# A filter's last chunk loaded as 128 half rows, fewer fillers ahead of the first transforms, and another fixed order

## The chip, the cores and the metric

The kernel runs on one core of one Trainium2 chip. The time is device microseconds of one execution, median of several. The kernel's engines are TensorE (PE, with its weight loads shown as PEld), VectorE (DVE), ScalarE (ACT), GpSimd (POOL) and SyncE (SP), which here only issues transfers; POOL issues transfers too, between its own arithmetic.

## The reference

A pre-norm block with two mixers over 2048 tokens (S) of 448 channels (D), all in bf16. The first is a gated long convolution, the second an MLP over the token axis.

```
def _A_ref(q, k, v, shift_k, ssm_k, ssm_D):
    k_shift = sum over t of k_pad[:, t:t+S] * shift_k[:, ks-1-t]     # 4 taps
    kv = k_shift * v
    kv_f = rfft2(pad(kv, 2S));  kf_f = rfft2(pad(ssm_k, 2S))          # over the token axis
    y = irfft2(kv_f * kf_f)[:, :S] + kv * ssm_D
    return q * y
def _B_ref(x, w1, b1, w2, b2):
    h = layernorm(x)
    u = gelu(einsum("bsd,sf->bdf", h, w1) + b1)
    return (einsum("bdf,fs->bds", u, w2) + b2).transpose(0, 2, 1)
h  = A_q + _A_ref(layernorm(A_q), k, v, shift_k, ssm_k, ssm_D)
h2 = h + _B_ref(layernorm(h), x, w1, b1, w2, b2)
```

The filter ssm_k is given channel by channel, 448 rows of 2048 samples; everything else has tokens as rows. F, the inner width of the MLP, is 1792.

## The kernel before

**Tiling.** Both Fourier transforms are matrix products in two stages, with a transposition between the stages done by transfers inside SBUF ("shuffles"). Tokens are split as 16 interleaved rows r with 128 positions each, so a tile is 128 partitions by 448 channels.

**Steps.** The builder functions write operations into a list; each operation has a name of the form step:number, and the steps are these.

- loads: all first transfers, on SP's queue (L885 on). loads.0 to loads.3 bring the filter's four chunks of 128, 128, 128 and 64 channel rows into KN (L887); loads.4 is the small shift kernel, loads.5 to 12 are quarters of k and v, loads.13 the vector D, loads.14 the two biases.
- tables: the cosine and sine tables, built from integers on DVE, ACT and POOL. tables.5 and tables.6 build E, the first stage's matrices, with three long DVE operations each (L844) and one on ACT. tables.7:0 to 7:3 are four integer operations on POOL (L854 three times, L858), 7:4, 7:6 and 7:7 are on DVE, 7:5 is a sine on ACT (L862), 7:8 to 7:11 are POOL's last steps (L871, L874). They give the second stage's matrices and masks.
- kv: kv.1 to kv.8 build transposes of k on PE (L966); kv.9 to kv.16 are the shift matmuls on PE (L992) followed by a DVE product with v (L1007).
- kT.2c+g: transposes of half g of filter chunk c, eight on PE (L1038) into one PSUM bank, and a copy to SBUF as :8 (L738 on ACT or L741 on DVE).
- dummy: matmuls on a constant tile that nobody reads (L1025): nine at the start (N_W0), and after each of the first three filter chunks N_WK of them, three, in one PSUM bank of their own.
- k1.0 to 15 and u1.0 to 15: the first stage of the transform of the filter and of kv: eight PE matmuls (L1059) and a copy (L1069, or L1067 with an addition of D on DVE), then after every second one three shuffles: :9 and :10 on POOL's queue, :11 on SP's (L1075). Every four steps share a slot of a ring of four; a slot is free once its shuffles have landed.
- k2, u2: the second stage, four matmuls (L1094) and one or two copies (L738, L739, L741, L742).
- i1: the product of the two spectra on DVE (L1160), the first inverse stage on PE (L1177), copies, and shuffles on POOL and SP (L1200; those of the last pair, i1.16, are issued at L1189).
- i2: the second inverse stage for 16 tiles (L1299, L1307 on PE), combined with q and the residual on DVE (L1318, L1326, L1336), layer norm statistics (L1342, L1345, L1374 on DVE, a power on POOL), and a scaling into Q, the MLP's input (L1385). i2.8 is that scaling for the first tile.
- mlp: the two products (L1432 and L1442 for the two halves of F, L1454 with w2), gelu on ACT (L1422), final additions on DVE (L1457). w1a and w1b (L1405, L1409) are the loads of w1's halves in four parts each.
- xload, xn, q, ct, ew, warm, bias: loads of x's rows and their statistics, transposes of the tables and more dummy matmuls.

**Order.** A fixed order for every engine is written out in ORDER, a list of such names for each of pe, act, dve, pool and sp. An engine issues its list in order, and SP's and POOL's lists are also the order of their transfer queues. Who copies what (ACT or DVE) is set by the list in which the copy stands. A planner walks these lists at build time and gives out the eight PSUM banks, the ring slots and the semaphores; whoever takes a bank waits for its last reader. Nothing is chosen at run time. Numbers as t0 and est below only serve that planner.

Of the kernel before, what the change touches and what calls it, by code (L numbers as in the profile page):

```python
# [13 lines left out]
        "dummy.0:1-9 kv.4:0-11 kv.3:0-7 kv.6:0-11 kv.5:0-7 kT.1:0-7 kT.0:0-3 kT.1:9-11 kT.0:4-7 kT.3:0-7 kT.2:0-3 "  # L14
        "kT.3:9-11 kT.5:0-7 kT.2:4-7 kT.5:9-10 kT.6:0-7 kT.7:0-7 bias.0:0 kT.5:11 kv.7:0-7 kv.2:0-3 k1.12:0-7 "
        "k1.8:0-7 k1.9:0-7 kv.2:4-11 kv.1:0-7 k1.10:0-7 k1.11:0-7 kT.4:0-7 kv.8:0-3 k1.13:0-7 k1.14:0-7 kv.8:4-11 "
        "kv.10:0-23 kv.12:0-23 kv.9:0-27 k1.4:0-7 k1.15:0-7 kv.11:0-27 u1.0:0-7 u1.1:0-7 k1.0:0-7 k1.1:0-7 u1.2:0-7 "
        "u1.3:0-7 kv.13:0-27 u1.4:0-7 k1.5:0-7 kv.14:0-23 k1.6:0-7 u1.6:0-7 u1.5:0-7 k1.2:0-7 kv.15:0-27 k1.7:0-7 "
        "u1.7:0-7 u1.8:0-7 u1.9:0-7 k1.3:0-7 k2.0:0-3 k2.1:0-3 k2.12:0-3 k2.13:0-3 k2.4:0-3 k2.5:0-3 kv.16:0-23 "
        "k2.9:0-3 k2.8:0-3 u1.10:0-7 u1.12:0-7 u1.13:0-7 u1.14:0-7 u1.11:0-7 u1.15:0-7 k2.2:0-3 k2.3:0-3 k2.7:0-3 "  # L20
        "k2.6:0-3 k2.10:0-3 k2.11:0-3 k2.14:0-3 k2.15:0-3 u2.0:0-3 u2.1:0-3 u2.12:0-3 u2.13:0-3 u2.8:0-3 u2.9:0-3 "
        "u2.6:0-3 u2.7:0-3 i1.1:1-7 i1.1:10-17 i1.1:8 i1.14:10-16 i1.14:1-7 i1.14:17 i1.14:8 i1.8:1-7 i1.8:10-16 "
        "i1.8:8 i1.8:17 ct0.0:0-7 u2.10:0-3 u2.11:0-3 i1.10:1 i1.10:10-17 i1.10:2-8 u2.5:0-3 u2.4:0-3 i1.12:1-8 "
        "i1.12:10-17 u2.3:0-3 u2.2:0-3 i1.6:1-8 i1.6:10-17 u2.14:0-3 u2.15:0-3 i1.4:9-15 i1.4:0-6 i1.4:16 i1.4:7 "
        "warm.12:0 warm.13:0 i1.16:1-7 i1.16:10-17 i1.16:8 ct.2:0-7 ct.1:0-7 ct.0:0-7 warm.0:0 warm.1:0 warm.2:0 "
# [557 lines left out]
def _build(nc, A_q, A_k, A_v, A_shift_k, A_ssm_k, A_ssm_D, B_w1, B_b1, B_w2, B_b2, out):  # L583
# [5 lines left out]
    Bsz, S, D = A_q.shape  # L589
    F = B_w1.shape[1]  # L590
    assert Bsz == 1 and S == 2048 and D == 448 and F == 1792 and A_shift_k.shape[-1] == 4
    R = 16
    NFC = F // 128
    EPS = 1e-5
    DB = 2 * D
# [42 lines left out]
    with ctx:  # L638
# [89 lines left out]
        T_KX = -27.67  # L728
        T_EW = -10.0
        T_CP, T_XL, T_WB = 39.11, -35.53, 156.06  # L730
        N_WZ, N_WI, N_W0, N_WK, N_WJ = 14, 0, 9, 3, 0

        def evac(dst, src, w, b, n, scale=None, engs=FX, r=(), est=None):

# [782 lines left out]
```

## Time and profile before

| | us |
|---|---|
| runs | 173.97, 173.15, 173.49; median 173.49 |
| the profiled execution, whole | 173.37 |
| its span | 171.6 |
| first load landed, last first load landed | 4.4, 19.5 |
| k2 starts | 34.7 |
| MLP starts | 81.4 |
| granted TensorE clock | 1.00 throughout |

The profile is of one execution. Times inside it count from the start of the span. A row of a timeline gives start, length, engine, line, operation, output and input, count, and in brackets the idle time of the engine ahead of it with whoever ended it. A window row gives for each engine the busy time and the number of instructions in that stretch. The chain of waits is followed back from the last instruction: at each step to what released it, or to the one before it on its engine. A busy PE here includes the dummy matmuls, so its share says little; what matters for each stage is which engine has no gap in it.

### The profile page before, as it was taken

What the parts mean: (1) busy time and instruction counts of PE and PEld (TensorE: products, weight loads), DVE (VectorE), ACT (ScalarE), POOL (GpSimd) and SP (SyncE); (2) the same over time, 40 slices, a digit from 0 to 9 for tenths busy, and PEclk for the clock granted to TensorE, in tenths of its full rate; (3) what the DMA queues carried; (4) which work ended last, traced back from release to release, by engine and by line L of the source; (5) the groups of instructions that cost most, each with busy time, mean ns of one, the idle gap of its engine ahead of it and who ended that gap; (6) DMA issues with size and microseconds to landing.
All of it is one profiled execution on the core that took longest, in us unless ns stands there. A gap on an engine that the chain in (4) does not pass through costs nothing.

```text
span 171.6 us, 3585 instructions
## 1 busy us (share of the span) xinstructions
PE 162.5 (95%) x1431; PEld 94.6 (55%) x1431; DVE 100.9 (59%) x187; ACT 92.6 (54%) x133; POOL 59.4 (35%) x152
## 2 busy tenths in 40 slices
PE   6989999989889999988999999999999999999994
PEld 2776745452324333533455455555567777777783
DVE  7998797879899999979997730000003133132231
ACT  3786978988999999978975816321210000000000
POOL 8345727564810696444898730000000000000000
PEclk9999999999999999999999999999999999999999
DMA  5999757676859776547989999980000111101111
GB/s 160 418 308 384 248 180 273 245 281 208 274 132 408 254 212 177 160 153 219 329 314 392 407 424 419 418 351 11 0 4 0 53 53 53 53 4 53 53 53 54
DMA packets 15628, 35.15 MB, mean 205 GB/s; under 512 B 3740, under 2 KB 9740, under 8 KB 15612
## 3 DMA queue, kind: packets, MB, share of 16 engines
q1 hardware_dynamic: 12468, 28.25, 45.3%
q0 software_dynamic: 2880, 6.49, 12.0%
q8 instruction: 11, 0.18, 0.4%
q10 hardware_dynamic: 264, 0.18, 0.3%
q14 instruction: 5, 0.04, 0.1%
HBM read 22.05 MB, written 1.84 MB: 139 GB/s over the span
## 4 chain that ended last, share of the span: by engine, by line
PE 67%; ACT 17%; DMA 7%; DVE 3%; POOL 2%; issue 2%; DVEq 0%; ACTq 0%
PE ps L1454 25%; ACT arena L738 13%; PE ps L1432 12%; PE ps L1442 12%; DMA arena<-arena 7%; PE ps L1025 3%; PE ps L1059 3%; PE ps L1094 3%; ACT arena L1069 3%; PE ps L966 3%; PE ps L1038 3%; PE ps L1299 2%; PE ps L992 2%; ACT arena L739 2%; POOL arena L1075 2%
## 5 line engine op out<-in xcount | busy, mean ns | idle before, releaser
L1457 DVE SCALAR_TENSOR_TENSOR arena<-ps,arena 128x448 bf16<-128x448 f32 (+2 forms) x17 | 11.1, 656 | 57.2 <-PE ps L1454 57.2
L1454 PE MATMUL ps<-arena 128*128 128x448 bf16 (+2 forms) x238 | 42.7, 342 | 0.0
L1454 PEld LDWEIGHTS ps<-arena 128*128 128x128 bf16 x238 | 33.3, 145 | 9.5
L738 ACT CAST arena<-ps 128x896 bf16<-128x896 f32 x30 | 24.5, 1006 | 0.3 <-PE ps L1094 0.2
L1432 PE MATMUL ps<-arena 128*128 128x448 bf16 x112 | 22.5, 353 | 0.6 <-DVE arena L1374 0.6
L1075 POOL DMA_DIRECT2D arena<-arena x32 | 17.5, 553 | 13.2 <-ACT arena L1069 9.9
L1069 ACT CAST arena<-ps 128x896 bf16<-128x896 f32 x23 | 19.5, 913 | 3.8 <-PE ps L1059 3.5
L1442 PE MATMUL ps<-arena 128*128 128x448 bf16 x112 | 21.4, 352 | 0.0
L1422 ACT ACTIVATE arena<-ps,arena 128x448 bf16<-128x448 f32 x14 | 8.2, 640 | 19.6 <-PE ps L1442 14.7
L1432 PEld LDWEIGHTS ps<-arena 128*128 128x128 bf16 x112 | 10.7, 98 | 11.3 <-DVE arena L1374 1.0
L1094 PE MATMUL ps<-arena 128*64 128x448 bf16 x128 | 15.1, 360 | 1.7 <-ACT arena L739 0.7
L1160 DVE TENSOR_TENSOR arena<-arena 128x1792 bf16<-128x1792 bf16 x16 | 16.6, 1085 | 0.3
L1442 PEld LDWEIGHTS ps<-arena 128*128 128x128 bf16 x112 | 11.0, 98 | 10.2
L1177 PE MATMUL ps<-arena 64*128 64x448 bf16 x128 | 14.7, 351 | 1.1 <-DVE arena L1160 0.7
L1059 PE MATMUL ps<-arena 128*32 128x448 bf16 x256 | 15.2, 355 | 0.5
L1200 POOL DMA_DIRECT2D arena<-arena x14 | 8.3, 596 | 13.2 <-ACT arena L738 13.2
L1094 PEld LDWEIGHTS ps<-arena 128*64 128x64 f16 x128 | 5.7, 108 | 10.3 <-ACT arena L738 3.2
L1177 PEld LDWEIGHTS ps<-arena 64*128 64x128 f16 x128 | 5.9, 94 | 9.7 <-DVE arena L1160 3.2
L738 ACT COPY arena<-ps 128x1024 bf16<-128x1024 bf16 (+2 forms) x9 | 8.3, 977 | 3.3 <-PE ps L966 2.8
L1007 DVE TENSOR_TENSOR arena<-ps,arena 128x512 bf16<-128x512 f32 (+1 forms) x16 | 9.0, 616 | 1.4 <-PE ps L992 1.4
L1354 ACT ACTIVATE arena<-arena 128x448 bf16<-128x448 f32 x14 | 8.0, 573 | 3.0 <-DVE arena L1326 2.9
L1059 PEld LDWEIGHTS ps<-arena 128*32 128x32 f16 x256 | 5.0, 95 | 7.9 <-ACT arena L1069 2.4
(96 smaller groups left out, 195.5 us busy)
## 6 DMA issues: line engine op xcount, KB each, us to landing
arena<-in_B_w_dram SPq DMA_DIRECT2D x8, 896.0 KB, 7.8
arena<-in_B_w_dram SPq DMA_DIRECT2D x2, 2048.0 KB, 17.6
arena<-arena SPq DMA_DIRECT2D x16, 224.0 KB, 3.0
arena<-arena POOLq DMA_DIRECT2D x32, 112.0 KB, 3.5
arena<-in_B_w_dram SPq DMA_DIRECT2D x2, 1536.0 KB, 20.1
arena<-arena POOLq DMA_DIRECT2D x14, 196.0 KB, 4.7
arena<-in_A_k_dram SPq DMA_DIRECT2D x4, 448.0 KB, 5.5
arena<-in_A_v_dram SPq DMA_DIRECT2D x4, 448.0 KB, 8.7
```

Of the source, the lines that this page charges most:

```text
L738: return e.copy(out=dst(), in_=src())
L1007: return e.tensor_tensor(out=v, in0=u.rearrange("p t (r d) -> p t r d", d=64), in1=v, op=ALU.mult)
L1059: op("pe", lambda e, W, b=b, r=r, q=q, x=x, c0=c0: e.matmul(PS[32 * q:32 * q + 32, b.slots[x], 0:D], E[:, 2 * r + x, c0:c0 + 32], src[:, r ...
L1069: return e.copy(out=dst, in_=Ppair(b)) if W == "act" else e.tensor_copy(out=dst, in_=Ppair(b))
L1075: shuf[tag].append(op(q_, lambda e, W, g=g, i=i, a=a, nu=nu, jh=jh: e.dma_start(T[a + i:a + i + 4 * nu - 3:4].rearrange("p (j k) c d -> p ...
L1094: op("pe", lambda e, W, b=bs[h], h=h, j=j, c=c, par=par: e.matmul(PS[64 * par:64 * par + 64, b.slots[c], 0:D], FW[:, 64 * c:64 * c + 64], ...
L1160: op("dve", lambda e, W, m=m, i=i: e.tensor_tensor(out=MR(m.slots[0]).rearrange("p (x y) d -> p x y d", x=2), in0=TU[:, i].unsqueeze(2).br ...
L1177: k = op("pe", lambda e, W, b=bs[h], m=ms[h], par=par, t=t, tab=tab, xy=xy, P=P: e.matmul(Pb(b, par), tab[P, :], MR(m.slots[0])[P, xy, :], ...
L1432: op("pe", lambda e, W, r=r, fc=fc, b=bs[fc]: e.matmul(Pb(b), W1A[:, r, 128 * fc:128 * fc + 128], Q[:, r, :], start=(r == 0), stop=(r == R ...
L1442: op("pe", lambda e, W, r=r, fc=fc, b=b: e.matmul(Pb(b), W1B[:, r, 128 * (fc - n0):128 * (fc - n0) + 128], Q[:, r, :], start=(r == 0), sto ...
L1454: op("pe", lambda e, W, r=r, fc=fc, b=b, d0=d0, d1=d1: e.matmul(Pb(b)[:, d0:d1], W2[fc // 7][:, fc % 7, r:S:R], G[:, fc, d0:d1], start=(fc ...
L1457: op("dve", lambda e, W, r=r, b=b, A=A, d0=d0, d1=d1: e.scalar_tensor_tensor(out=X[:, r, d0:d1], in0=Pb(b)[:, d0:d1], scalar=bm[:, r:r + 1 ...
```

## The change

Five things.

1. The filter's last chunk, 64 channel rows of 2048 samples, is loaded as 128 half rows of 1024 (row 2c holds the first half of channel c, row 2c+1 the second). For each r there are now two matmuls in place of one transpose: the half rows, 128 partitions by 64 samples, are the stationary operand, and every second column of the identity is the moving one, so one matmul gives positions 0 to 63 and the other 64 to 127. The result is f32 in PSUM (a whole bank of 512), where the transposes left bf16.
2. The fillers between the filter chunks: three after each of three chunks become one after the first alone. Four new ones (fill.0 to fill.3) have a PSUM bank each from the planner and no reader.
3. w1a.0, the first quarter of w1's first half, no longer waits for u1's shuffles but for a landed z shuffle (that of i1.8), and stands further back in SP's list, behind the last pair's shuffles.
4. Some copies change engine: k2.13's second, kT.4's, kv.6's, u1.9's, one of u2.13's and of u2.3's, and i2.98, go to DVE; bias.0's, k1.14's, kT.7's, u1.7's, one of u2.1's and of u2.5's, and i2.94, go to ACT.
5. All five lists are in another order. Among the moves: tables.5's first step is DVE's first long one; POOL's tables.7:0 to 7:3 move from before the first shuffle to between k1.11's and k1.13's, tables.7:8 to 7:11 to between k1.5's and u1.5's; k1.14 and k1.15 stand ahead of kv.9, kv.10 and kv.12 on PE; the loads start with a quarter of k and filter chunks 0 and 2; on DVE, i2.14 and i2.55 stand ahead of i2.8; on PE, i2.58 stands ahead of the MLP's first product.

The lists are cut here to the parts named above; the code is whole.

```diff
 "pe":
-  "dummy.0:1-9 kv.4:0-11 kv.3:0-7 kv.6:0-11 kv.5:0-7 kT.1:0-7 kT.0:0-3 kT.1:9-11 kT.0:4-7 kT.3:0-7 kT.2:0-3 "
-  "kT.3:9-11 kT.5:0-7 kT.2:4-7 kT.5:9-10 kT.6:0-7 kT.7:0-7 bias.0:0 kT.5:11 kv.7:0-7 kv.2:0-3 k1.12:0-7 "
-  "k1.8:0-7 k1.9:0-7 kv.2:4-11 kv.1:0-7 k1.10:0-7 k1.11:0-7 kT.4:0-7 kv.8:0-3 k1.13:0-7 k1.14:0-7 kv.8:4-11 "
-  "kv.10:0-23 kv.12:0-23 kv.9:0-27 k1.4:0-7 k1.15:0-7 kv.11:0-27 u1.0:0-7 u1.1:0-7 k1.0:0-7 k1.1:0-7 u1.2:0-7 "
+  "dummy.0:1-9 kv.5:0-6 kv.6:0-3 fill.0:0 kT.1:0-7 kT.1:9 kT.0:0-7 kv.6:4-11 kT.5:0-7 bias.0:0 kv.5:7 "
+  "fill.1:0 fill.2:0 fill.3:0 kv.4:0-11 kT.6:0-15 kT.7:0-15 kv.3:0-7 kT.3:0-7 kT.2:0-7 kv.7:0-7 k1.8:0-7 "
+  "k1.12:0-7 k1.9:0-7 kv.1:0-7 kv.2:0-3 k1.10:0-7 kv.2:4-11 k1.11:0-7 k1.13:0-7 kT.4:0-7 kv.8:0-3 k1.14:0-7 "
+  "k1.15:0-7 kv.8:4-11 kv.12:0-23 kv.9:0-27 kv.10:0-23 k1.4:0-7 kv.11:0-27 k1.0:0 u1.0:0-7 u1.1:0-7 k1.0:1-7 "
...
 "dve":
-  "xn.3:1 i2.4:0 i2.11:0 i2.5:0 i2.18:0 i2.6:0 i2.12:0 i2.21:0 i2.13:0 q.7:1 i2.8:0 i2.14:0 i2.55:0 i2.30:0 "
+  "i2.12:0 i2.6:0 i2.13:0 i2.18:0 i2.14:0 i2.21:0 i2.55:0 i2.8:0 i2.16:0 i2.34:0 i2.30:0 i2.43:0 i2.26:0 "
...
 "pool":
-  "tables.2:6 q.0:0-1 kv.0:1-2 tables.7:0-3 tables.7:8-11 kv.0:0 k1.9:9-10 k1.11:9-10 k1.13:9-10 k1.15:9-10 "
-  "u1.1:9-10 u1.3:9-10 k1.1:9-10 k1.5:9-10 u1.5:9-10 k1.3:9-10 k1.7:9-10 u1.7:9-10 u1.9:9-10 u1.13:9-10 "
+  "tables.2:3 tables.2:0 tables.2:7 tables.2:10 tables.2:8 tables.2:11 kv.0:0 kv.0:2 tables.2:6 k1.9:9-10 "
+  "k1.11:9-10 tables.7:2 tables.7:1 tables.7:0 tables.7:3 k1.13:9-10 k1.15:9-10 u1.1:9-10 k1.1:9-10 u1.3:9-10 "
+  "k1.5:9-10 tables.7:8 tables.7:10 tables.7:9 tables.7:11 u1.5:9-10 k1.3:9-10 k1.7:9-10 u1.7:9-10 u1.9:9-10 "
...
 "sp":
-  "loads.6:0 loads.8:0 loads.0:0 loads.1:0 loads.2:0 loads.3:0 loads.13:1 loads.14:0-1 loads.10:0 loads.5:0 "
-  "loads.11:0 loads.4:0-2 loads.12:0 loads.9:0 loads.7:0 k1.9:11 k1.11:11 k1.13:11 k1.15:11 u1.1:11 k1.1:11 "
+  "loads.8:0 loads.0:0 loads.2:0 loads.14:0 loads.6:0 loads.3:0 loads.1:0 loads.10:0 loads.4:2 loads.4:1 "
+  "loads.4:0 loads.5:0 loads.14:1 loads.11:0 loads.7:0 loads.9:0 loads.13:1 loads.12:0 k1.13:11 k1.15:11 "
...
-  "w1a.0:0 xload.3:0 xload.2:0 ct0.1:0 i1.1:20 i1.1:22 ct0.1:1 ct0.1:4 ct0.1:2 ct0.1:5 ct0.1:3 i1.16:22 "
-  "i1.16:19-20 i1.4:21 i1.4:19 i1.10:20 i1.8:20 w1a.1:0 i1.6:20 i1.6:22 i1.8:22 i1.14:22 w1a.2:0 w1a.3:0 "
+  "i1.16:19-20 i1.14:22 w1a.0:0 i1.12:20 i1.10:22 i1.10:20 i1.8:20 i1.8:22 w1a.1:0 i1.1:22 w1a.2:0 i1.14:20 "
...
-        N_WZ, N_WI, N_W0, N_WK, N_WJ = 14, 0, 9, 3, 0
+        N_WZ, N_WI, N_W0, N_WK, N_WJ = 14, 0, 9, 1, 0
...
-            for i, c in enumerate((0, 1, 2, 3)):
-                sch.t0 = -20.0 + i
-                op(Dq, lambda e, W, c=c: e.dma_start(KN[0:CW[c], c, :], A_ssm_k[128 * c:128 * c + CW[c], :]),
-                   w=[(o_KN + 4096 * c, 4096)], dmab=CW[c] * 4096, rate=217.0 if c == 3 else None)
+            for c in range(3):
+                sch.t0 = -20.0 + c
+                op(Dq, lambda e, W, c=c: e.dma_start(KN[:, c, :], A_ssm_k[128 * c:128 * c + 128, :]),
+                   w=[(o_KN + 4096 * c, 4096)], dmab=128 * 4096)
+            sch.t0 = -17.0
+            op(Dq, lambda e, W: e.dma_start(
+                KN[:, 3, 0:S // 2], A_ssm_k[384:448, :].rearrange("c (h s) -> (c h) s", h=2)),
+               w=[(o_KN + 4096 * 3, 2048)], dmab=128 * 2048)
...
+        def emit_fill():
+            for i in range(4):
+                b = _Buf(psum)
+                sch.t0 = -50.0 + i
+                op("pe", lambda e, W, b=b: e.matmul(Pb(b), DUM[:, 0:128], DUM, start=True, stop=True),
+                   r=[(o_DUM, DB)], bw=[b], n=D)
...
-                        k = op("pe", lambda e, W, b=b, rr=rr, r=8 * g + rr, c=c, cw=cw: e.transpose(
-                            out=Pbf(b, 0)[:, rr * cw:rr * cw + cw], in_=KN[0:cw, c, r:S:R], identity=ID[0:cw, 0:cw]),
-                            r=[(o_KN + 4096 * c, 4096), (o_ID, 256)], bw=[b], kind="tr", mode=4 if c == 3 else 0,
-                            safter=(k,) if c == 3 and rr == 0 else ())
+                        if c < 3:
+                            k = op("pe", lambda e, W, b=b, rr=rr, r=8 * g + rr, c=c: e.transpose(
+                                out=Pbf(b, 0)[:, rr * 128:rr * 128 + 128], in_=KN[:, c, r:S:R], identity=ID),
+                                r=[(o_KN + 4096 * c, 4096), (o_ID, 256)], bw=[b], kind="tr")
+                            continue
+                        for h in range(2):
+                            k = op("pe", lambda e, W, b=b, rr=rr, r=8 * g + rr, h=h: e.matmul(
+                                PS[64 * h:64 * h + 64, b.slots[0], 64 * rr:64 * rr + 64], KN[:, 3, r:S // 2:R],
+                                ID[:, h:128:2], start=True, stop=True),
+                                r=[(o_KN + 4096 * 3, 2048), (o_ID, 256)], bw=[b], est=20.0, mode=2,
+                                safter=(k,) if rr == 0 and h == 0 else ())
...
-                if i < 3:
+                if i < 1:
                     dummy(N_WK, T_KT + 1.0 * (2 * i + 1), (k,))
...
-                       after=shuf["zl"] if h else shuf["u"], safter=(wl[0],) if h else ())
+                       after=shuf["zl"] if h else [shuf["zpool7"]], safter=(wl[0],) if h else ())
```

## The prediction

> **What bounds the kernel now.** I read the page's first parts, then busy time by stage, then the chain of waits, then the timelines of the engines that the chain names. The median of the runs is 173.49 us; the profiled execution took 173.37, 171.6 of it span and 1.8 around it. All sums below are against 173.37.
>
> ```profile
> PE 162.5 (95%) x1431; PEld 94.6 (55%) x1431; DVE 100.9 (59%) x187; ACT 92.6 (54%) x133; POOL 59.4 (35%) x152
> PEclk9999999999999999999999999999999999999999
> PE 67%; ACT 17%; DMA 7%; DVE 3%; POOL 2%; issue 2%; DVEq 0%; ACTq 0%
> ```
>
> PE is busy 95% of the span, but on only 67% of the chain: dummy and warm matmuls count as busy. The windows (columns: stretch, length, then busy time and count of PE, PEld, DVE, ACT, POOL, then granted clock, DMA share, GB/s) say which engine sets each stage.
>
> ```profile
> 4.20:13.40 9.20, 8.68 (x114) 6.85 (x113) 9.12 (x20) 7.64 (x7) 3.60 (x11) 1.00 1.04 368
> 13.40:22.40 9.00, 9.00 (x202) 6.06 (x201) 7.62 (x11) 6.27 (x9) 5.46 (x11) 1.00 0.93 316
> 34.70:47.50 12.80, 11.78 (x146) 5.02 (x148) 11.04 (x12) 11.46 (x14) 8.82 (x17) 1.00 0.77 263
> 47.50:70.40 22.90, 21.25 (x191) 8.41 (x189) 22.59 (x29) 22.86 (x29) 9.70 (x17) 1.00 0.74 231
> 81.40:105.40 24.00, 24.00 (x127) 12.21 (x128) 16.56 (x46) 15.20 (x38) 15.85 (x38) 1.00 0.99 378
> ```
>
> To 13.4 the DVE is full (9.12 of 9.20), to 22.4 the PE; from 47.5 to 70.4 the ACT has no gap (22.86 of 22.90); from 81.4 the PE has none. What the change moves lies before 81.4. The chain of waits (start, length) there:
>
> ```profile
> 22.39 0.91 ACT arena L1069
> 23.32 4.06 DMA arena<-arena
> 30.74 3.90 DMA arena<-arena
> 34.73 0.96 PE ps L1094 x8
> 47.55 13.62 ACT arena L738 x17
> 71.20 4.38 DMA arena<-arena
> 76.97 0.68 DVE arena L1336
> 81.39 0.92 PE ps L1432 x4
> ```
>
> The first two rows are k1.15's copy and its shuffle: the landing (28.13 for the last half) frees a ring slot, and u1.4's copy on ACT starts at 28.20. The third is k1.5's shuffle, whose landing starts k2 at 34.73; then copies until kv.16, which lets u1.12 start on ACT at 40.40. From there ACT copies back to back to 70.33, the last z shuffle lands at 75.58, and DVE turns the first output tile into Q, with which the token MLP starts at 81.39. So two things count: when u1.12 starts, and how long from the last landing to the first MLP matmul.
>
> **The change, part by part.** *Four fillers less.* Nine fillers become one, and four new ones with a bank each come: 9 → 5, at the 0.19 us that a warm one takes (three in 0.58), 0.77 us less PE work. They lay beside a full DVE, and the chain had 1.53 us of them:
>
> ```profile
> 7.58 0.73 PE L1025 MATMUL ps<-arena 128*128 128x448 bf16 x3
> 11.68 1.18 PE L1038 MATMUL ps<-arena 64*128 64x64 bf16 x16
> 13.86 1.32 PE L1059 MATMUL ps<-arena 128*32 128x448 bf16 x24
> 8.35 0.68 DVE L741 COPY arena<-ps 128x1024 bf16<-128x1024 bf16 x1
> ```
>
> They are not free fillers all: the planner gives fill.1 the bank of kT.0, so it waits for kT.0's copy on DVE. That copy stands behind the tables: their long operations now begin with tables.5:0 and end near 8.27 (8.43 now), the copy takes 0.68, so PE waits from about 7.75 to 9.0. The 1.25 us idle are the fillers' place taken by a wait. Behind it in PE's order: three fillers to 9.57, kv.4's twelve transposes at 56 ns to 10.23, kT.6 and kT.7, kv.3, kT.3.
>
> *Half rows.* The 16 transposes of 64 rows (1.11 us on the chain, 69 ns each) become 32 matmuls with 64 columns. No row has one; the nearest are those 69 ns above, and half of a 128-column transpose, 28 ns, below: 0.9 to 2.2 us. I take 38 ns, 1.2 us, nearer the lower end because rows of 128 columns go at 56 back to back. So kT.7 ends at 11.45, kv.3 11.9, kT.3 12.35, its copy on DVE 13.33, and k1.8 starts at 13.37 instead of 14.25. At 69 ns the lead is gone and the front term below is zero. The Trainium skill ("TensorE: Matmul & The Clock Gate", Part 3) says that matmuls in different column groups of the array run side by side, and the two halves write partitions 0–63 and 64–127; the L1059 row above agrees, 24 matmuls of 448 columns in four groups in 1.32 us, 55 ns each where a full one takes 190. By it the 32 would cost like 16, 0.6 us, kT.7 would end 0.6 earlier, and the front would still stop at the bound that DVE's copies before kv.16 set below; so it adds to the faster rival's chance alone. Both copies now read f32; kT.7's goes to ACT, 0.6 us there, beside a wait. The load has the same 256 KB in 128 rows; its 1.26 us as 64 rows equals a 512 KB chunk's 1.25, so it saves some 0.6 of a load stream that ends at 19.5 and isn't on the chain.
>
> *The order in front.* ACT's k1.8 copy comes 0.88 earlier (14.05). k1.12 on DVE stays at 14.55; kv.12 gains 0.38, kv.11 0.63; k1.11's copy ends at 17.57 (18.41 now), k1.15's at 19.98 (23.29), since k1.14 and k1.15 go ahead of the shift products on PE. POOL is what keeps most of this gain from arriving. Its queue now:
>
> ```profile
> 7.42 2.05 POOL L854 TENSOR_SCALAR arena<-arena 128x128 int32<-128x128 int32 x3 [2.67 <-DVE arena L831]
> 9.55 1.01 POOL L858 TENSOR_TENSOR arena<-arena 128x384 int32<-128x384 int32 x1
> 18.70 2.15 POOL L1075 DMA_DIRECT2D arena<-arena  x4 [0.38 <-ACT arena L1069]
> 23.58 1.08 POOL L1075 DMA_DIRECT2D arena<-arena  x2 [2.73 <-ACT arena L1069]
> ```
>
> The four L854/L858 operations (2.05 + 1.01, 3.1 us) move behind k1.11's two issues and ahead of k1.13's and k1.15's: k1.11's end at 18.95, the tables at 22.1, k1.13's issues at 23.2, k1.15's at 24.25 against 24.66. Of 3.3 us that k1.15's copy gains, 0.4 is left. Behind them wait u1.1, k1.1 and so on; each still issues no later than now. The landing follows the issue by 3.47 now: 27.7, u1.4 0.4 earlier, k2.0 at 34.35. By the transfer records the POOL shuffles between 16 and 34 us land in two groups, near 2.8 and at 4.0 to 4.6 us after their issue, the slow ones where a 16 KB instruction packet lies beside them (at 24.4, one that took 1.44 us). With the short landing u1.4 is 1.2 earlier and k2.0 1.1.
>
> From k2.0 on, DVE now has three copies and kv.16's products in a row (1.09 ×3 + 1.01, as k2.13's copy came over from ACT), where it waited 0.82 for PE: kv.16's end is 39.5 (now 39.65) with the slow landing, 38.7 with the short one. That is −0.14 to −0.95 for u1.12; I take −0.5, between, as both kinds of landing occur. From 40.4 to 70.3 ACT makes 36 copies, as now (one to DVE, one back), so the shift goes through to the last landing whole.
>
> *The second inverse stage.* Now DVE starts Q's scaling 3.87 us after the first L1336 (76.97 to 80.84), the MLP at 81.38. In the new order i2.14 and i2.55 stand ahead of that scaling (i2.8), which come right behind it now: a small variance step and the L1318 copy of a later tile (0.68), while one small step leaves: +0.7. Two i2.58 matmuls (0.38), now inside the MLP's run, go before it into the wait: −0.4. Net +0.3, bounds 0 and +0.7.
>
> *Weights.* w1a.0, now issued at 49.7 and landed at 57.2, moves on SP's queue behind the last pair's shuffle issues, about 74.7. w1a.1's took 4.94 (77.26 to 82.20): 79.6, 2 us before the MLP needs it; by the page's median of 7.8 it is 82.5, 0.6 too late. SP's shuffles of i1.4, i1.8 and i1.10 that stood ahead are behind it now; what they move is read by the last two tiles alone, long after 82. I cost it at 0, bounds 0 and +0.8.
>
> *Sum:* −0.5 + 0.3 = −0.2: 173.2. Its own range is 172.6 to 174.2: front −0.95 to 0, second stage 0 to +0.7.
>
> **The rivals.** *Short landing, gain carried (faster).* Front −0.95 and the second stage at its lower bound: 172.4; with the front's full −1.2, 172.2. For it: most shuffles land in 2.8; moved instructions move the packets. Against it: DVE's row of copies before kv.16.
>
> *POOL's tables hold the ring (slower).* One mechanism: 3.1 us of table work ahead of k1.13's and k1.15's shuffles. It decides once k1.11's copy ends after about 18.0: at the present 18.41 the tables end at 22.9, k1.15's issues at 25.1, the landing is at 28.6 and u1.4 0.4 late; with a slow landing of 4.6 it is 1.2 late. With the second stage's +0.3 to +0.7: 174.1 to 175.3, I say 174.6. For it: k1.8's lead hangs on the unseen half-row price and on the wait at 9 us. Against: 0.88 of lead by the walk.
>
> *The clock falls.* Without fillers the front has, from 6.3 to 9.0, small transposes and 1.25 us of idle. Should the clock be at half until full matmuls have run again, some 4 us of PE work to 13.4 would take 8: 177. Against it: from 4.61 to 7.58 the PE ran 52 transposes and nothing else, 2.97 us, with the clock at 1.00. The same page of the Trainium skill (Part 4) says that transposes don't count as busy for the clock; those 2.97 us are within its window of about 3.4 us, so this trace can't refute it.
>
> *It doesn't do what it says.* The four free fillers wait for a copy; then they neither hold the clock nor save anything: this is in the forecast already, at zero.
>
> **How the numbers follow.** Forecast 0.42, faster 0.31, POOL 0.17, late weights 0.05 (173.8 to 174.6), clock 0.05. A change under 0.5%, 0.87 us, I count as none: 172.6 to 174.4. The faster rival and little else lies under it: 0.32. Above it are most of POOL's, the clock's and some of the weights' and the forecast's own edge: 0.27. Range 171.8 to 175.2, from the faster rival's best to POOL's worst.
>
> **What would show it.** PE idle some 1.2 us near 8 to 9 with kT.0's copy as releaser; 32 half-row matmuls in 1.2 us; k1.8's copy on ACT starting near 14.1; POOL's tables at 19 to 22 and k1.15's issues ending at 24.2; u1.4 near 27.8, k2.0 near 34.3, u1.12 near 39.9; ACT full for 29.9 us from there; 4.4 to 5.1 us from the first L1336 to the first L1432. The forecast is wrong if u1.12 starts before 39.4 or after 40.6, if MLP waits for w1a.0, or if the clock row shows under 9 after 5 us.

## The result, and the profile after

The changed kernel takes 175.47 us (median of 6 runs, 175.04 to 176.36) against 173.29 for the kernel before (6 runs, 173.15 to 173.97): a ratio of 1.0128, 95% interval 1.0096 to 1.0160. That is slower by 2.2 us, where 0.2 less was forecast, and outside the forecast's range. The profiled execution took 176.16 with a span of 174.35, so it is one of the longer ones: the 2.8 us by which its span exceeds the old one (171.56) are 0.6 more than the medians say.

Line numbers have moved: the first stage's copies are L1087 and L1089 (were L1067, L1069), its shuffles L1095 (L1075), the half-row matmuls L1057, k2 L1114 (L1094), the first combination of the last stage L1356 (L1336), the MLP's first product L1452 (L1432). First lines from the page of the changed kernel, then its windows (columns as in the prediction): the stretches shown of before where they still cut a stage, otherwise shifted with it, and one more, 26.0 to 30.5. The last fence has that stretch of the kernel before.

```profile
PE 162.9 (93%) x1443; PEld 94.8 (54%) x1443; DVE 101.8 (58%) x187; ACT 92.1 (53%) x133; POOL 58.0 (33%) x152
PEclk9999999999999999999999999999999999999999
PE 65%; DVE 13%; ACT 10%; DMA 5%; issue 3%; POOL 2%; DVEq 0%; POOLq 0%; ACTq 0%
```

```profile
4.20:13.40 9.20, 8.30 (x113) 6.66 (x112) 7.43 (x14) 5.76 (x6) 1.30 (x6) 1.00 1.04 401
13.40:22.40 9.00, 9.00 (x195) 6.33 (x195) 7.22 (x13) 8.12 (x10) 4.45 (x8) 1.00 0.59 208
26.00:30.50 4.50, 3.22 (x68) 1.49 (x64) 2.96 (x7) 3.54 (x5) 1.72 (x4) 1.00 0.46 173
42.90:72.90 30.00, 27.45 (x261) 10.29 (x255) 28.61 (x36) 29.50 (x37) 13.96 (x25) 1.00 0.63 197
84.50:108.00 23.50, 23.50 (x125) 12.12 (x125) 16.34 (x46) 14.72 (x36) 14.50 (x36) 1.00 1.04 393
```

```profile
26.00:30.50 4.50, 4.38 (x104) 2.52 (x100) 3.24 (x5) 3.83 (x5) 3.54 (x7) 1.00 0.79 285
```

The busy times are nearly those of before (162.5, 94.6, 100.9, 92.6 and 59.4), and the ends of the program look alike: ACT is full for the 30 us from u1.12 on (29.50 busy; 29.45 of 29.90 before) and PE for the MLP. The new thing is the third row. From 26.0 to 30.5 no engine is full (PE is busy for 3.22 of 4.50 us, 4.38 before) and the DMA engines are busy less than half the time (0.46, 0.79 before). Everybody waits, and the chain of waits there shows for what:

```profile
27.49 0.24 DVE arena L1087
27.73 0.77 issue
28.49 1.08 DVE arena L1087
29.86 0.86 POOL arena L1095 x2
31.85 3.77 DMA arena<-arena
...
35.69 2.55 ACT arena L1089 x3
38.24 0.83 ACT arena L741
...
42.92 3.33 ACT arena L1089 x4
...
73.74 4.29 DMA arena<-arena
...
79.42 0.68 DVE arena L1356
```

It goes through k1.0's and k1.1's copies on DVE (L1087), which weren't on the chain before, to u1.3's shuffle. Its landing at 35.62 frees a ring slot for u1.8's copy on ACT (35.69); two more first-stage copies and the first of k2's (38.24) stand behind that one. k2's own start at 37.14, with k1.5's landing at 37.01, lies beside this chain and is as late. The timelines of DVE, of the changed kernel and of the one before (start, length, engine, line, operation, and in brackets the idle time ahead), show the same pair of copies:

```profile
27.49 2.09 DVE L1087 TENSOR_TENSOR arena<-ps,arena 128x896 bf16<-128x896 f32 x2 [1.76 <-PE ps L1079]
```

```profile
24.85 2.09 DVE L1067 TENSOR_TENSOR arena<-ps,arena 128x896 bf16<-128x896 f32 x2 [0.15 <-PE ps L1059]
```

The pair starts 2.64 us later, and DVE idles 1.76 us ahead of it. The bracket names PE, but k1.0's matmuls ended at 25.90. The bracket misleads here; what ended the wait was a transfer. k1.0 is the first to write a ring slot for the second time, so it needs the shuffles of k1.9 and k1.11 out of that slot. Of the three shuffles of a pair SP's moves 224 KB and POOL's two 112 KB each; the texts on record below call SP's the half. The transfer records give (issue, landing) for the four that go over SP's queue:

| shuffle on SP | before | after |
|---|---|---|
| k1.9 | 16.67, 20.07 | 22.72, 27.41 |
| k1.11 | 18.44, 21.13 | 22.08, 24.66 |
| k1.13 | 19.36, 24.41 | 19.72, 23.12 |
| k1.15 | 23.32, 27.37 | 21.47, 23.94 |

SP's new list has them as k1.13, k1.15, k1.11, k1.9. k1.9's copy was done at 16.84, but SP stood at k1.13 until 19.72 and at k1.15 until 21.47. k1.9's shuffle on SP was issued at 22.72 and landed at 27.41, DVE's sequencer stood at a wait for it from 24.74 to 27.44, and k1.0's copy began at 27.49.

From there the delay goes down the line: k1.0's copy +2.64, k1.5's last shuffle issue +2.18 (30.74 to 32.92), its landing +2.38, k2 +2.41 (34.73 to 37.14), u1.12's copy +2.52, the last z shuffle's landing +2.44, the first combination +2.45 (76.97 to 79.42). From the first combination to the end of the last addition on DVE (169.50 before, 172.29 after) it is 92.53 before and 92.87 after. 2.45 + 0.34 is the whole 2.79 between the two profiles.

### The profile page after: what moved, and what is told of

Same layout as the page of the kernel before. It is cut to its first block, busy times and chain, and to the rows that moved or that the text cites. A ratio compares the mean times of both kernels' runs of the same rounds, so it can differ in the third digit from the quotient of the medians.

```text
span 174.3 us, 3617 instructions
## 1 busy us (share of the span) xinstructions
PE 162.9 (93%) x1443; PEld 94.8 (54%) x1443; DVE 101.8 (58%) x187; ACT 92.1 (53%) x133; POOL 58.0 (33%) x152
## 4 chain that ended last, share of the span: by engine, by line
PE 65%; DVE 13%; ACT 10%; DMA 5%; issue 3%; POOL 2%; DVEq 0%; POOLq 0%; ACTq 0%
PE ps L1474 24%; PE ps L1452 12%; PE ps L1462 12%; DMA arena<-arena 5%; ACT arena L1089 4%; ACT arena L740 4%; PE ps L1079 3%; PE ps L1197 3%; DVE arena L1180 3%; PE ps L1114 3%; PE ps L1319 2%; PE ps L972 2%; DVE arena L1013 1%; ACT arena L741 1%; DVE arena L846 1%
## 5 line engine op out<-in xcount | busy, mean ns | idle before, releaser
L740 ACT CAST arena<-ps 128x896 bf16<-128x896 f32 (+2 forms) x33 | 25.8, 935 | 1.3 <-PE ps L1057 0.9
L1089 ACT CAST arena<-ps 128x896 bf16<-128x896 f32 x24 | 20.5, 911 | 5.3 <-PE ps L1079 4.2
L1095 POOL DMA_DIRECT2D arena<-arena x32 | 17.6, 556 | 14.7 <-ACT arena L1089 12.4
L1452 PE MATMUL ps<-arena 128*128 128x448 bf16 x112 | 22.3, 353 | 0.0
L1462 PE MATMUL ps<-arena 128*128 128x448 bf16 x112 | 21.4, 353 | 0.0
L1079 PE MATMUL ps<-arena 128*32 128x448 bf16 x256 | 15.7, 356 | 2.6 <-DVE arena L1087 1.0
L1452 PEld LDWEIGHTS ps<-arena 128*128 128x128 bf16 x112 | 10.9, 98 | 10.4 <-DVE arena L1405 0.3
L1114 PE MATMUL ps<-arena 128*64 128x448 bf16 x128 | 15.0, 360 | 1.5 <-ACT arena L740 0.8
L1114 PEld LDWEIGHTS ps<-arena 128*64 128x64 f16 x128 | 5.4, 108 | 10.3 <-ACT arena L740 3.2
L1405 DVE TENSOR_SCALAR arena<-arena 128x448 bf16<-128x448 f32 x16 | 7.7, 507 | 3.0 <-POOL arena L1398 2.9
L1319 PE MATMUL ps<-arena 128*128 128x448 bf16 x32 | 7.7, 353 | 1.5 <-DVE arena L1338 1.0
```

The lines of the kernel that those rows point to most:

```text
L740: return e.copy(out=dst(), in_=src())
L1079: op("pe", lambda e, W, b=b, r=r, q=q, x=x, c0=c0: e.matmul(PS[32 * q:32 * q + 32, b.slots[x], 0:D], E[:, 2 * r + x, c0:c0 + 32], src[:, r ...
L1089: return e.copy(out=dst, in_=Ppair(b)) if W == "act" else e.tensor_copy(out=dst, in_=Ppair(b))
L1095: shuf[tag].append(op(q_, lambda e, W, g=g, i=i, a=a, nu=nu, jh=jh: e.dma_start(T[a + i:a + i + 4 * nu - 3:4].rearrange("p (j k) c d -> p ...
L1114: op("pe", lambda e, W, b=bs[h], h=h, j=j, c=c, par=par: e.matmul(PS[64 * par:64 * par + 64, b.slots[c], 0:D], FW[:, 64 * c:64 * c + 64], ...
L1319: k = op("pe", lambda e, W, b=b, r=r, h=h: e.matmul(Pb(b), ET[:, 2 * r + h, :], TZ[:, r, h, :], start=(h == 0), stop=(h == 1 and r >= NZ)) ...
```

## The experiments

Each was run beside the kernel before on the same chip; ratios are to that, with a 95% interval. "Whole rows" below means the last filter chunk loaded and transposed as before the change.

### SP's order of the first shuffles

Theory S: SP's order is the loss. Rivals: H, the half rows on PE; P, POOL's tables ahead of k1.13's and k1.15's shuffles. "A shuffle on SP" is the one of the three that goes over SP's queue. First the changed kernel with these four as before:

```diff
-  k1.13:11 k1.15:11 k1.11:11 k1.9:11 u1.1:11
+  k1.9:11 k1.11:11 k1.13:11 k1.15:11 u1.1:11
```

> The changed kernel with one edit: on SP's list the first four shuffles stand as before (k1.9, k1.11, k1.13, k1.15) and no longer with k1.9's last (issued at 22.72, landed at 27.41 in the changed kernel's trace). Theory S, SP's order holds the first ring slot: k1.0's copy starts when kv.11's products end, near 25.8 instead of 27.5, u1.4's copy near 28.2 (29.3), k2 some 1.5 to 2 us earlier than 37.1; time 173.4 to 174.0. Rival H, the front is late by the half rows on PE and the wait for kT.0's copy: the slot is no limit of its own, k2 moves by less than 0.4, time 175.1 to 175.5. Rival P, POOL's tables ahead of k1.13's and k1.15's shuffles: k1.0 moves but u1.4 waits for k1.15's landing at 28.2 or later, and k2 gains only what lies between, under 1 us; time 174.5 to 175.

174.64 us, ratio 1.0043 (1.0022 to 1.0064). Its DVE timeline:

```profile
25.98 2.09 DVE L1087 TENSOR_TENSOR arena<-ps,arena 128x896 bf16<-128x896 f32 x2 [0.28 <-PE ps L1079]
```

k1.0's copy starts 1.51 us earlier, u1.4's at 28.51, k2 at 35.52, 1.62 earlier. Theory S holds for its part, in the size expected; the time itself is above the expected 173.4 to 174.0, 0.5 us of that because the kernel before took 173.79 beside these runs and not 173.29. By the time alone rival P's 174.5 to 175 would fit, but it allowed k2 less than 1 us, and u1.4's copy started right behind the copy ahead of it on ACT and not at k1.15's landing (28.18). Against 1.0128 this one edit gives back 0.85%, 1.5 of the 2.2 us.

The same swap the other way, in the kernel before:

```diff
-  k1.9:11 k1.11:11 k1.13:11 k1.15:11
+  k1.13:11 k1.15:11 k1.11:11 k1.9:11
```

> The kernel before with SP's first four shuffles in the changed kernel's order (k1.13, k1.15, k1.11, k1.9). Theory S: k1.15's copy ends at 23.29, k1.9's half is issued near 25 and lands at 28 to 29.5, k1.0's copy moves from 24.85 to there, k2 by 2.5 to 4 us; time 175.8 to 177.5. Rivals H and P: SP's order alone costs nothing, 173.2 to 173.6.

176.2 us, ratio 1.0137 (1.0090 to 1.0183). In its profiled execution the granted clock was 0.99, so only the place of the waits is read from it. k1.0's copy, due at the end of kv.11's products (25.77), waits for a transfer:

```profile
29.51 2.09 DVE L1067 TENSOR_TENSOR arena<-ps,arena 128x896 bf16<-128x896 f32 x2 [3.74 <-DMA arena<-arena]
```

It isn't the transfer that theory S had in mind. The planner reckons with SP's list when it gives out the ring slots, and in this build it gave them the other way round: the semaphores on which k1.0's copy waits are those of k1.13's and k1.15's shuffles, the last of them k1.15's on POOL (issued 25.19, landed 29.48). k1.9's shuffle on SP is issued as late as 25.65, lands at 30.30, and holds u1.4's copy instead (30.37). So four names in another order on one queue cost the old kernel 2.4 us, but that is the price of the order and of the planner's answer to it together. In the changed kernel and in a_sp_order k1.0's copy waits for k1.9's and k1.11's shuffles, so the comparison of those two is free of it.

### The half rows

> The changed kernel with the filter's last chunk as 64 whole rows again (its load and its 16 transposes; order, fillers and copies as changed). Theory H: the 32 matmuls took 2.09 us where 16 transposes took 1.11, so all behind them on PE comes 1 us earlier, k1.8 near 13.5, and the end with it; time 174.4 to 174.7. Theory S: k1.15's copy hangs on ACT's row of copies, and SP's issues on that; if ACT's row moves by the whole 1 us, the slot does too and the two theories give the same; if it moves by less because its first copies wait for tables, 174.7 to 175.4.

The edit puts back the load and the transposes of the last chunk (the diff of the change, backwards, for that part). 174.57 us, ratio 1.0052 (1.0029 to 1.0074), below the 174.7 to 175.4 that theory S allowed and inside H's range. Against 1.0128 the whole rows alone give back 0.76%, 1.3 us, almost as much as SP's order alone. Its profiled execution was its longest (175.86), so its lengths say little of the typical run, but it shows the place of the wait:

```profile
26.70 2.09 DVE L1076 TENSOR_TENSOR arena<-ps,arena 128x896 bf16<-128x896 f32 x2 [1.58 <-DMA arena<-arena]
```

k1.0's copy still waits for k1.9's shuffle on SP (issued 23.04, landed 26.62), and that stands behind k1.15's, whose copy on ACT ends at 20.84 here and at 21.44 in the changed kernel. So the half rows and SP's order delay the same transfer, and the 0.85% and 0.76% that each gives back alone are in part the same time: both undone together give back 0.69% (below).

> The kernel before with the half rows alone (load, 32 matmuls, copies of f32), in its own order. Theory H: 1.0 us more PE work on the chain at 11.7 to 12.9, carried through k1.12 and k1.8 to k2: time 173.9 to 174.4. Theory S: the ring slot of k1.15 sets u1.4 and k1.15's copy comes behind a PE row without gaps from 13.4 to 22.4, so the 1 us is carried as well unless it falls into a wait: 173.3 to 174.3. A price under 0.3 says that the half rows are no part of the loss.

The half rows alone in the kernel before: 174.6 us, ratio 1.0052 (1.0030 to 1.0074), 0.9 us slower. H's 173.9 to 174.4 had been reckoned from 173.29, 0.6 to 1.1 more. Its PE timeline (that of the kernel before is in the prediction, 16 in 1.18):

```profile
11.65 2.13 PE L1048 MATMUL ps<-arena 128*64 128x64 bf16 x32
```

kT.7 ends at 13.78 instead of 12.86, k1.15's copy at 24.23 instead of 23.29, k2 starts at 35.59. A matmul of a half row takes 65 ns from one to the next (2.08 us for 32 in the changed kernel), hardly less than a transpose of the 64 whole rows (69 ns), so twice the matmuls cost almost twice the time.

### What is left with both undone

SP's order and whole rows together should have brought the time back to the kernel before.

> The changed kernel with SP's first four shuffles as before and the last filter chunk as whole rows: what is left of the change is the other order, the fillers, w1a.0 and the copies' engines. Theory S and H together: the two losses add, k2 starts 0.6 us earlier than the 35.5 with SP's order alone, near 34.9, the MLP's start keeps its +0.35; ratio 0.999 to 1.002 to the kernel before. Rival, a third cost in the front (POOL's tables, the wait at 9 us): k2 stays at 35.4 or later, ratio 1.003 or more.

174.99 us, ratio 1.0059 (1.0037 to 1.0082): a miss. It is no better than with SP's order alone. All up to k1.5 did come earlier than there (its matmuls by 0.8 us, its copy at 29.05 instead of 29.57, its last shuffle's issue at 30.78 instead of 31.40), yet k2 started at 35.73. The chain of waits:

```profile
29.98 0.54 SPq L1084
30.52 0.04 issue
30.56 4.97 DMA arena<-arena
35.53 0.20 issue
35.73 0.96 PE ps L1103 x8
```

The transfer at 30.56 is k1.1's shuffle on SP: its copy was done at 27.28, but SP's list has it behind k1.5's, which SP could issue only at 29.98. This is the first fault a second time. Three variants of this kernel were run beside it:

```diff
a_sp_full_i2, DVE:
-  i2.18:0 i2.14:0 i2.21:0 i2.55:0 i2.8:0 i2.16:0
+  i2.18:0 i2.8:0 i2.14:0 i2.21:0 i2.55:0 i2.16:0
a_sp_full_nofill, PE:
-  fill.1:0 fill.2:0 fill.3:0 kv.4:0-11
+  kv.4:0-11
a_sp_full_pool, POOL (tables.4:20 moves up on DVE as well):
-  tables.2:6 k1.9:9-10 k1.11:9-10 tables.7:2 tables.7:1 tables.7:0 tables.7:3 k1.13:9-10
+  tables.2:6 tables.7:2 tables.7:1 tables.7:0 tables.7:3 k1.9:9-10 k1.11:9-10 k1.13:9-10
```

> The one before, with i2.8 (the scaling into the first Q) ahead of i2.14, i2.21 and i2.55 on DVE. The trace of the changed kernel has POOL's power for it done at 82.69 and i2.8 at 84.00, behind two long operations, and PE idle from 83.16 to 84.14. Theory: i2.8 comes 1.2 us earlier relative to the first L1356, PE's idle 1 us goes, the MLP ends 0.6 to 1.0 earlier than without this edit; ratio 0.994 to 0.998. Rival, Q of the second tile is late next because i2.14 and POOL's second power slip: under 0.3 of gain.

Ratio 1.0070 (1.0050 to 1.0090), no gain. i2.8 did start 1.7 us earlier (80.85 for 82.56), and the MLP started where it had (83.06, 83.13): on PE i2.58 stands ahead of it, and i2.58's bank is freed by i2.55, the step that now came later.

```profile
82.67 0.55 PE L1308 MATMUL ps<-arena 128*128 128x448 bf16 x2 [1.40 <-DVE arena L1327]
```

The wait only changed its name.

> The first of this set without fill.1 to fill.3 (three dummy matmuls, 0.57 us). kv.4 then takes kT.0's bank and waits for the same copy. Theory W (the wait, not the fillers, is what PE spends there, and three fillers behind it are on the path): k1.8 0.5 earlier, k2 as much or, where ACT's copies bind, 0.3; ratio 0.996 to 1.000. Rival C, the clock falls without them: the granted clock in the stretch from 9 to 14 is under 1.0 and the time 1 to 4 us longer.

Ratio 1.0047 (1.0015 to 1.0079). The interval covers both the expected gain and none at all; k1.8 came 0.26 earlier, not 0.5, and k2 at 35.67. What it does settle is the clock. With two fillers behind the first dummies, both before 8 us, the granted clock stays at 1.00:

```profile
4.20:9.00 4.80, 4.59 (x43) 3.33 (x42) 4.70 (x8) 2.61 (x2) 0.94 (x3) 1.00 1.05 358
9.00:14.00 5.00, 5.00 (x86) 4.32 (x88) 4.31 (x10) 4.37 (x6) 0.36 (x3) 1.00 1.03 350
```

> The first of this set with POOL's four table operations (tables.7:0 to 7:3) back ahead of k1.9's shuffle, where POOL was idle from 5 to 12, and the small DVE step that feeds them (tables.4:20) moved up. Rival P, they hold the ring slot: k1.13's and k1.15's issues come 2 us earlier, u1.4's copy too as far as ACT lets it; k2 0.4 or more earlier. Theory S: once k1.9's half is in time, u1.4's copy stands behind u1.3's on ACT (27.7 to 28.6) and the slot is free at about the same time, so k2 moves by less than 0.3; the ratio is that of the first of this set within 0.002.

Ratio 1.0034 (1.0015 to 1.0053). POOL's issues for k1.13 and k1.15 come 2.2 and 1.9 us earlier (19.44 and 20.92), the last of k1.15 lands at 24.55 instead of 28.18, and the ring slot that this rival is about is free 3.6 us earlier. The 0.42 us for which ACT stood idle ahead of u1.4's copy in a_sp_full are gone (27.73 instead of 28.24), but k2 starts at 35.74, as without the edit: k1.5's last shuffle lands at 35.60, and at 35.38 in a_sp_full. So the tables hold a slot a little, as rival P has it, and k2 doesn't depend on it once k1.9's shuffle on SP is in time. Whether the 0.25% between the ratios of this and a_sp_full are anything, their intervals don't say.

### The second fault, and PE's order

```diff
a_sp2_full, SP:
-  u1.1:11 u1.3:11 k1.5:11 k1.1:11
+  u1.1:11 k1.1:11 u1.3:11 k1.5:11
a_sp2_full_k17, also PE and ACT:
-  u1.9:0-7 k1.7:0-7 k2.0:0-3 k2.1:0-3        k1.7:8 k2.1:4
+  u1.9:0-7 k2.0:0-3 k2.1:0-3 k1.7:0-7        k2.1:4 k1.7:8
```

> SP's first four shuffles as before, whole rows, and also k1.1's half ahead of u1.3's and k1.5's on SP, as before the change. Without this last edit it stood behind k1.5's, was issued at 30.56 though its copy was done at 27.28, landed at 35.53 and released k2 at 35.73. Theory S2, the same mistake a second time: the half lands near 29.6, k1.5's shuffles land earlier too (34.4 to 34.8), and k2 starts as soon as PE comes to it. PE has k1.7 ahead of k2.0, which ended at 35.41: so 35.4 to 35.5, 0.2 to 0.3 earlier, ratio 1.003 to 1.005. Rival: the transfers as a whole are the limit and k2 stays at 35.7.

Ratio 1.0065 (1.0033 to 1.0098). In the profile k1.1's shuffle on SP is no longer what k2 waits for; k1.5's last shuffle lands at 34.80, and k2 starts at 35.20, behind k1.7 on PE. The mechanism is as expected, the time doesn't show it.

> The one before with k1.7's matmuls and copy behind k2.0 and k2.1 (k2.0 and k2.1 don't read k1.7's output). Theory O, the order of PE from 28 to 35 is the third cost of the front: k2.0 starts at k1.5's landing, 34.5 to 34.9, and the end comes 0.5 to 0.9 earlier than without this edit; ratio 0.998 to 1.002. Rival, k2's copies, or u1.7's and u1.9's shuffles, which now stand behind a later k1.7 on POOL, take it back: u1.12's copy stays at 41.2 or later.

Ratio 1.0064 (1.0029 to 1.0099). k2 starts with k1.5's landing (35.07, k2 at 35.16), but u1.12's copy comes at 41.58, later than without the edit (40.98): the late k1.7 takes the place of k2's own copies. The rival of this run was right.

### The order in the last stage

```diff
b_i2after, the kernel before:
-  DVE: q.7:1 i2.8:0 i2.14:0 i2.55:0          PE: mlp.0:2 mlp.0:4 mlp.0:3 mlp.0:0 i2.58:0-1
+  DVE: q.7:1 i2.14:0 i2.55:0 i2.8:0          PE: i2.58:0-1 mlp.0:2 mlp.0:4 mlp.0:3 mlp.0:0
b_i2opt, the kernel before, DVE:
-  i2.12:0 i2.21:0 i2.13:0 q.7:1 i2.8:0 i2.14:0 i2.55:0
+  i2.12:0 i2.13:0 i2.8:0 i2.14:0 i2.21:0 q.7:1 i2.55:0
```

> The kernel before with the changed order in the second inverse stage alone: i2.14 and i2.55 ahead of i2.8 on DVE, i2.58 ahead of the MLP's first matmul on PE. Theory from the forecast: +0.7 on DVE, 0.4 back on PE, so 0.3 slower, ratio 1.001 to 1.003. Rival: nothing, since DVE's later tiles come earlier for it, within 0.001.

Ratio 1.0026 (0.9996 to 1.0057): in line with +0.3 us, though the interval reaches to nothing. From the first combination to the end of the last addition the profile has 92.87 us (77.70 to 170.57), 0.34 more than before and the same as in the changed kernel.

> The kernel before with i2.13, i2.8 and i2.14 ahead of i2.21 on DVE. In the trace of before POOL's power for i2.8 is done at 80.26 and PE idle from 80.77 to 81.38. Theory: i2.8 starts near 80.35, the MLP near 80.9, PE's idle 0.6 us goes and the end comes 0.4 to 0.6 earlier, ratio 0.996 to 0.998. Rival: Q of the second tile, or the bank that i2.21 frees, is late next, and the gain is under 0.2.

Ratio 1.0041 (1.0013 to 1.0069), slower where 0.4 to 0.6 of gain was hoped for. The MLP does start 3.9 us after the first combination instead of 4.4. Then it stops twice:

```profile
81.49 0.93 PE L1373 MATMUL ps<-arena 128*128 128x448 bf16 x4
82.82 0.55 PE L1240 MATMUL ps<-arena 128*128 128x448 bf16 x2 [0.39 <-DVE arena L1259]
83.21 0.62 PE L1373 MATMUL ps<-arena 128*128 128x448 bf16 x2
84.08 0.74 PE L1373 MATMUL ps<-arena 128*128 128x448 bf16 x3 [0.25 <-ACT arena L1257]
```

The PSUM bank that i2.55 frees on DVE (L1259) is late next, and then one that a step of the same kind frees on ACT (L1257). The wait of 0.6 us ahead of the MLP is bought back by a row without stalls behind it.

### Grafts: the old order from one point on

To find where the last 0.6% lie, the front of the changed kernel (both SP faults undone, whole rows) got the old lists, and w1a.0's old wait, from u1.12 on (a_tail40) or from behind k1.5's copy on (a_tail28); a_tail28_half is the latter with the half rows.

> The changed order with SP's two swaps undone and whole rows (ratio 1.0065) up to u1.10; from u1.12 on, all five lists and w1a.0's wait as before. If the later stages' order is what remains: the MLP starts 4.4 us after the first combination instead of 5.1 with i2.58 inside, 0.3 us; and ACT's row from 40 to 70 and the rest no better; ratio 1.003 to 1.005. If they hold the whole rest: 1.000 to 1.002. If none of it: 1.006.

Ratio 1.0036 (1.0021 to 1.0051).

> The same front up to k1.5's matmuls and copy (about 28 us), from there all five lists as before. Theory O, the order from 28 to 40 holds the rest: k2 starts at k1.5's landing, 34.6 to 35.3, u1.12's copy 5.7 us later as in the kernel before; ratio 0.997 to 1.001, faster than before if the front's lead of 0.8 us at k1.5's copy arrives. Rival L, the shuffles' landing doesn't follow their issue (34.6 to 35.6 in all runs so far, for issues from 30.4 to 31.5): the lead is lost and the ratio is 0.999 to 1.003. Rival F, the cost is in the front after all: 1.004 or more.

Ratio 1.0023 (1.0004 to 1.0042).

> The one before with the half rows. Theory H: all up to k1.5 comes 0.8 us later, k1.5's shuffles are issued at 31.4 instead of 30.6, and k2 and the end come 0.5 to 0.9 later than in a_tail28. Rival L: the landing stays at about 35 and the price is under 0.3.

Ratio 1.0065 (1.0040 to 1.0089).

a_tail28 and a_tail28_half differ in the half rows alone: 0.42%, 0.7 us, with intervals that just touch. That is the price of the half rows in the new front, beside 0.9 in the old one. Their PE timelines:

```profile
10.59 1.15 PE L1048 MATMUL ps<-arena 64*128 64x64 bf16 x16
```

```profile
10.40 2.08 PE L1058 MATMUL ps<-arena 128*64 128x64 bf16 x32
```

Between them k1.8 starts at 13.67 and 14.41, k2 at 35.44 and 36.02. The old order from u1.12 on takes the ratio from 1.0065 to 1.0036, as much as the last stage's 0.3 us and some room for error; the old order from 28 us on adds little that the intervals can tell.

No version run was faster than the kernel before.

## Why the prediction was wrong, point by point

**The front, −0.5 forecast, about +2 measured: the step that failed.** It is the paragraph on the order in front: "POOL is what keeps most of this gain from arriving", and "each still issues no later than now". POOL's queue was walked shuffle by shuffle and SP's wasn't, though one of every three shuffles is SP's and the new list of SP moves k1.9's and k1.11's behind k1.15's. Two rows of the trace of before would have done: k1.9's shuffle on SP issued at 16.67, and k1.15's at 23.32. With the forecast's own end of k1.15's copy, 19.98, and the 1.25 us from k1.15's issue to k1.9's in the changed kernel, k1.9's would go at about 21.2 and land 3.4 to 4.7 us later, at 24.6 to 25.9 (an estimate), when k1.0's copy was due at 24.2 by the same walk (24.85 less the 0.63 that it gives kv.11). The walk then took only k1.15's landing (u1.4's copy) as a limit of the ring, and passed over the first slot, which k1.0 needs and which in the trace of before was free only 1.4 us ahead of its use (k1.11's last landing 23.47, k1.0's copy 24.85). a_sp_order shows it: −0.85% when undone, k1.0's copy 1.51 us earlier. The rest of the loss in front isn't SP's list alone: k1.15's copy ended at 21.44 and not at 19.98, and with whole rows (a_full_rows) it ends at 20.84, so 0.60 of that lies with the half rows in that profile. b_sp_order has +1.37% for the list in the old kernel, there with other ring slots too.

**Half rows: the second step that failed, a size.** 38 ns were taken within 28 to 69; 65 was measured, 2.08 us for 32 and not 1.2. The text had the upper end and said what it does (no lead, the front's gain zero). That was too little: the doubled matmuls cost 0.7 and 0.9 us of the end in two orders without the fault on SP, and 1.3 in the changed kernel with it.

**The four fillers and the wait.** fill.1 does wait for kT.0's copy, as walked. PE came to that wait at 8.69, behind bias.0 and kv.5's last transpose, and not at 7.75, and the copy ended at 9.20, not 8.95, so PE's idle time was 0.57 us and not 1.25. Removing three of the fillers changed nothing that could be told from noise.

**POOL's tables.** They ran from 20.29 to 22.52 (19 to 22 forecast), k1.15's last issue ended at 24.68 (24.25), and its landing was at 28.15, the slow one of the two. Nothing waited for it long, and moving them away gave k2 nothing. The rival that had the right sign had the wrong queue; that its 174.6, at worst 175.3, comes near the result is chance.

**The short landing.** The faster rival needed the shuffles to land 2.8 us after their issue. k1.15's took 4.02 from the start of its last issue, k1.5's 4.09.

**From u1.12 to ACT's last copy.** 29.9 us forecast from u1.12's copy to i1.4's last, 29.94 measured (42.92 to 72.86). Right.

**The last stage.** +0.3 forecast, +0.34 measured in the profile of the changed kernel and +0.34 with that order alone. 5.14 us from the first combination to the first MLP matmul (79.42 to 84.56), just over the upper end of 4.4 to 5.1. Right, the mechanism too: i2.8 starts 4.58 us after the first combination (79.42 to 84.00) instead of 3.87, and i2.58's 0.38 lies in the wait.

**w1a.0.** Issued at 77.59, landed at 84.12, 0.4 us ahead of the MLP's start at 84.56. Cost nothing, as forecast, though the landing took 6.53 us and not 4.9; had the front come out as forecast, the margin should have been about the same, since its issue shifts with the z shuffles.

**The clock.** 1.00 throughout, with five fillers and with two, and 0.57 us of idle PE at 9 us. In a_sp_full_nofill PE ran nothing but transposes from 7.98 to 13.35 us. The reading of the Trainium skill ("TensorE: Matmul & The Clock Gate", Part 4) that transposes wouldn't hold the clock isn't borne out over these 5 us; a longer stretch of transposes was in no run.

**The sums.** The nine fillers on the chain come to 1.82 us, not 1.53 (a last one of 0.29 at 12.97 was left out). A front of −0.95 to 0 and a second stage of 0 to +0.7 give 172.4 to 174.1, not 172.6 to 174.2, and 171.8 lies below the faster rival's best of 172.2. None of this brings the forecast nearer to 175.47.

**What stays open.** The parts add up to more than the whole: 1.5 us for SP's order, 0.7 to 0.9 for the half rows, 0.34 for the last stage make 2.5 to 2.7 where the medians differ by 2.2. Parts hide behind each other: with SP's order mended, going back to whole rows gained nothing until the old order stood behind it as well. Some 0.6% remain with both undone. In a_sp2_full's profile the chain to u1.12 doesn't pass k2's start: it comes through three first-stage copies on ACT, and k2's first copy behind them starts at 36.30 where the kernel before has it at 35.69; u1.12's is then at 40.98 (40.40). Moving one of the three back (a_sp2_full_k17, 41.58) or the whole order (a_tail28, 41.14) didn't bring 40.40, so the order there isn't shown as the cause. Why a_tail28 is still at 1.0023, though its front is 0.6 ahead at k1.8 and level at k1.5's shuffles, wasn't settled; its k2 waits for a copy on ACT that ended at 35.40, not for the landing at 35.24.

## What to carry to other kernels

A transfer queue that runs in program order is an engine of its own: when an order changes, walk it like the others, and for each entry ask when the one ahead of it can go, not when its own data are ready. A ring has as many limits as slots; the one that is not on today's chain may have only a microsecond or two of slack. Where a planner reckons with the order, a swap can also move buffers to other slots: look which transfer a wait is for before comparing. And what an engine is seen to wait for last in a profile need not be what released it: when the engine named was done long before, look at the landings.

## What the runs showed of the hardware

In these rows the price of small matmuls doesn't fall with their size: 56 ns for a 128-column transpose, 69 for one of 64 rows, 65 for a half-row matmul with 64 columns. In the same kernel the first stage's matmuls of 448 columns, in four column groups, go at 52 ns (24 in 1.25 us). So the rule of the Trainium skill ("TensorE: Matmul & The Clock Gate", Part 3) that column groups run side by side agrees with the trace for those (a full one of 448 columns takes 190), but for 64 columns in two groups no gain can be seen: 2.08 us, where the prediction's estimate by that rule was 0.6. Weight loads filled 1.98 of the 2.09 us there; whether they are the limit wasn't tested.

The landing of a shuffle follows its issue only loosely. k1.5's last shuffle in the fourteen profiles with the old order of SP's first shuffles and a full clock (start of the issue, landing, start of k2):

| kernel | issue | landing | k2 |
|---|---|---|---|
| before | 30.74 | 34.63 | 34.73 |
| b_i2after (same front) | 30.52 | 35.32 | 35.41 |
| b_i2opt (same front) | 31.07 | 35.25 | 35.34 |
| a_sp_full_nofill | 30.39 | 35.21 | 35.67 |
| a_sp_full_pool | 30.63 | 35.60 | 35.74 |
| a_sp_full | 30.78 | 35.38 | 35.73 |
| a_sp_full_i2 | 30.91 | 35.19 | 35.28 |
| a_sp2_full | 30.63 | 34.80 | 35.20 |
| a_sp2_full_k17 | 30.63 | 35.07 | 35.16 |
| a_tail40 | 30.72 | 34.69 | 35.11 |
| a_tail28 | 30.69 | 35.24 | 35.44 |
| a_sp_order | 31.40 | 34.80 | 35.52 |
| a_tail28_half | 31.42 | 35.85 | 36.02 |
| b_half_rows | 31.47 | 35.49 | 35.59 |

The issues lie within 1.1 us and the landings within 1.2, with little order between them, and the same front in three executions gives 34.63 to 35.32. A lead of some tenths ahead of such a transfer is worth nothing that one profile could show; only medians over many runs tell.
